# Attention and a cosine feed-forward layer on one core: the short matmuls of a tile in two runs instead of four, and the last rows stored in two halves

## The chip, the cores and the metric

The kernel runs on one core of one Trainium2 chip. Its engines work side by side, each through its own list of instructions in order: TensorE (PE, matmuls, with weight loads as PEld), VectorE (DVE), ScalarE (ACT), GpSimd (POOL) and SyncE (SP, which issues the DMAs here). They wait for each other by semaphores. The metric is device time in microseconds (us): the median of several executions.

## The reference

Chunked attention over 8 batches, 8 heads, 576 positions in chunks of 64, head size 64, and then a feed-forward layer on the result (4608 tokens of 512, inner size 2048), all in float32:

```python
scores = scale * np.matmul(q_c, k_c.transpose(0, 1, 2, 4, 3))   # chunks of 64 x 64
scores = scores - np.max(scores, axis=-1, keepdims=True)
attn = np.exp(scores)
attn = attn / (np.sum(attn, axis=-1, keepdims=True) + 1e-09)
out = np.matmul(attn, v_c)
...
x = np.ascontiguousarray(attn_out.transpose(0, 2, 1, 3)).reshape(B * S, H * D)
...
h = x @ w_in
g = h * np.cos(h)
return (g @ w_out).astype(np.float32)
```

## The kernel before

The 4608 tokens are cut into nine tiles of 512. For each tile, the feed-forward layer goes through sixteen steps, one for each block `fc` of 128 inner columns. To keep float32 precision, every large operand is split into a high and a low part, and three products are added up. A step has these parts:

- `hidden(t, fc)` on TensorE: twelve matmuls of 128 x 512 into a PSUM bank named `h`. The pool `ps_h` has two such banks, used in turn.
- `activated`: six operations, alternately on ScalarE (lines 497, 499, 501) and VectorE (498, 500, 502). They read the bank `h`, form g = h cos h and split it into `g_hi` and `g_lo`. The multiplication in line 500 is the last reader of the bank.
- `project(s)` on TensorE: twelve matmuls that multiply `g` by `w_out` into four banks `acc`, one for each 128 rows (`sub`). It runs LAG = 3 steps behind `hidden`. After the sixteenth step of a tile `finish` copies the four banks out, alternately on ScalarE and VectorE, and stores them.

While a tile goes through its sixteen steps, the attention of the tile after it is worked out in between (`attend`). The eight heads form four pairs `hp` = 0 to 3, and two pairs form a group `g`. The scores of a group are 32 matmuls of 64 x 64, the weighted sums of a group are 32 more. The trace shows two records for each of these short matmuls. They write the two banks `a0` and `a1` (pool `ps_a`); the other six of the eight PSUM banks are `acc` and `h`. The stations of a tile's attention are:

- steps 0 and 1: scores of group 0, then of group 1 (`scores`). The matmuls stand between `hidden` and `project` of the step. VectorE then takes the largest of each row (line 363) and subtracts it (line 367), which empties the banks.
- step 2: exponentials on ScalarE (line 376). Steps 3 to 6: sums and quotients on VectorE.
- steps 4 to 7 and 9 to 12: the weights of each pair are transposed into tiles `pts` by eight VectorE instructions (`turned`, line 422).
- steps 8 and 13: weighted sums of group 0, then of group 1 (`weighted`). ScalarE (line 460) and VectorE (line 463) split the result into the parts `x` that `hidden` reads for the next tile.

The loads for the tile after are issued by SP in program order: values of pairs 2 and 3 at step 9, queries, keys and the other values from step 13 (`prefetch`).

The order of the work comes from two places. The first two and a half tiles (the list `work`, STAGE = 32 steps) are ordered by a planner with estimated durations. From then on a plain loop at the end of the kernel calls the functions; each engine gets its instructions in the order of the calls. Three queues of small pieces hold back work of VectorE and ScalarE: `activate` takes pieces of `soon` and `full` between its own operations, and empties `full`, `soon` and `late`, in that order, at its end. The loop covers the attention of the fourth to ninth tile.

Of the kernel before, what the change touches and what calls it, by code (L numbers as in the profile page):

```python
# [11 lines left out]
F32 = mybir.dt.float32  # L12
# [9 lines left out]
P = 128  # L22
TOK = 512
CH = 64
BL = 32
LAG = 3
# [3 lines left out]
SHIFT = 28  # L30

GROUP = 8

EARLY = 2

# [123 lines left out]
def attention_then_cos_ffn(ctx: ExitStack, tc, qT, kT, v, w_in, w_out, out, wide):  # L159
# [5 lines left out]
    NT, HP = qT.shape[0], qT.shape[1]  # L165
    NFC, NCC = w_in.shape[1], w_in.shape[2]
    DM = out.shape[1]
    NCH = TOK // CH
    NSUB = TOK // P
# [22 lines left out]
    def matmul(*args, **kw):  # L192
        kept(nc.tensor.matmul(*args, **kw))  # L193
# [101 lines left out]

    def load_v(t, hp):

        if t or hp < 2:
            vt = att.tile([P, TOK], F32, name="vt")
        else:  # L300
            if hp == 2:
                values["roomy"] = x_room(1, F32)
            vt = values["roomy"][:, hp - 2]
        load(vt, v[t, hp])
        values[t, hp] = vt

    def bank(kind, i):
        if kind == "a":
            b = ps_a.tile([P, 512], F32, name=f"a{i % 2}")
        else:  # L310
            b = ps_o.tile([P, 512], F32, name=f"acc{i}")
        return b

    def weights_of(t, g):
        if ("e", t, g) not in probs:
            probs["e", t, g] = att.tile([P, 2, NCH, CH], F32, name=f"e{g}", bufs=1)
        return probs["e", t, g]
# [23 lines left out]
    def scores(t, g, banks):  # L341

        for j in range(2):
            qt, kt = queries.pop((t, 2 * g + j))
            for c in range(NCH):
                pr, par = divmod(c, 2)
                cs, ps = slice(c * CH, (c + 1) * CH), slice(par * CH, (par + 1) * CH)
                o = (j * NPR + pr) * CH  # L350
                for h in range(2):
                    hs = slice(h * CH, (h + 1) * CH)
                    matmul(
                        banks[h][ps, o : o + CH], qt[hs, cs], kt[hs, cs], start=True, stop=True
                    )
        e = weights_of(t, g).rearrange("p a (r h) k -> p a r h k", h=2)
        found = []
        for h in range(2):
            sv = banks[h].rearrange("p (a r k) -> p a r k", a=2, k=CH)
            m = att.tile([P, 2, NPR], F32, name="m", bufs=4)  # L360

            def largest(m=m, sv=sv):
                kept(nc.vector.tensor_reduce(out=m, in_=sv, op=ALU.max, axis=AX.X))

            def below(m=m, sv=sv, h=h):
                mb = m.unsqueeze(3).broadcast_to([P, 2, NPR, CH])
                kept(nc.vector.tensor_tensor(e[:, :, :, h], sv, mb, op=ALU.subtract))  # L367

            found.extend((largest, below))
        return found  # L370
# [41 lines left out]

    def turned(t, hp):

        pts = att.tile([P, TOK], F32, name="pts")
        probs[t, hp] = pts
        src = weights_of(t, hp // 2)[:, hp % 2].rearrange("p c (x k) -> p c x k", k=BL)
        dst = pts.rearrange("p (c x q) -> p c x q", x=CH // BL, q=BL)

        def piece(par, qb, kb):  # L420
            i, o = (par * CH + x * BL for x in (qb, kb))
            kept(nc.vector.transpose(out=dst[o : o + BL, :, qb], in_=src[i : i + BL, :, kb]))  # L422

        nb = CH // BL
        return [
            lambda x=(par, qb, kb): piece(*x)
            for par in range(2) for qb in range(nb) for kb in range(nb)
        ]

    def weighted(t, hps, banks):  # L430


        g, first = divmod(hps[0], 2)
        n = len(hps)
        for j, hp in enumerate(hps):
            pts = probs.pop((t, hp))
            vt = values.pop((t, hp))
            for pr in range(NPR):
                for par in range(2):
                    ks = slice(par * CH, (par + 1) * CH)  # L440
                    o = (j * NPR + pr) * CH
                    for h in range(2):
                        hs = slice(h * CH, (h + 1) * CH)
                        fs = slice((2 * pr + h) * CH, (2 * pr + h + 1) * CH)
                        matmul(
                            banks[par][hs, o : o + CH], vt[ks, fs], pts[ks, fs],
                            start=True, stop=True,
                        )
        if (t, g) not in x_parts:
            x_parts[t, g] = tuple(x_room(t, F32R) for _ in range(2))  # L450
        splits = []
        for par in range(2):
            xq = banks[par][:, : n * TOK // 2].rearrange("p (a r q) -> p a r q", a=n, q=CH)
            hi, lo = (
                x[:, first : first + n].rearrange("p a (r c q) -> p a r c q", c=2, q=CH)[:, :, :, par]
                for x in x_parts[t, g]
            )

            def high(xq=xq, hi=hi):
                kept(nc.scalar.copy(out=hi, in_=xq))  # L460

            def rest(xq=xq, hi=hi, lo=lo):
                kept(nc.vector.tensor_tensor(lo, xq, hi.bitcast(F32), op=ALU.subtract))  # L463

            splits.extend((high, rest))
        return splits
# [52 lines left out]
    def project(s):  # L519
        t, fc = order[s]  # L520
        first = s == 0 or order[s - 1][0] != t
        last = s == len(order) - 1 or order[s + 1][0] != t
        g_hi, g_lo = g_parts.pop((t, fc))
        w_hi, w_lo = w_parts["out", fc]
        sums_out = []
        for sub in range(NSUB):
            if first:
                acc[sub] = bank("acc", sub)
            o = acc[sub]
            ss = slice(sub * P, (sub + 1) * P)  # L530
            matmul(o, g_hi[:, ss], w_hi, start=first, stop=False)
            matmul(o, g_hi[:, ss], w_lo, start=False, stop=False)
            matmul(o, g_lo[:, ss], w_hi, start=False, stop=last)
            if last:
                sums_out.append(lambda sub=sub, o=o: finish(t, sub, o, fc == NFC - 1))
        return sums_out

    def out_room(sub):

        return (wts if sub % 2 else dec).tile([P, DM], F32, name=f"half{sub // 2}" if sub % 2 else "w")  # L540

    def finish(t, sub, o, whole):
        r0 = t * TOK + sub * P
        to = out[r0 : r0 + P, :]
        if not whole:

            os, to = att.tile([P, DM], F32, name="vt" if sub % 2 else "pts"), partial[sub]
        elif t == 0:
            os = acc["partial", sub]
        elif t < NT - 1:  # L550
            os = out_room(sub)
        else:
            if sub % 2 == 0:
                acc["last"] = x_room(t + 1, F32)
            os = acc["last"][:, sub % 2]
        if whole and t == 0:
            kept(nc.vector.tensor_tensor(os, os, o, op=ALU.add))
        elif sub % 2 == 0:
            kept(nc.scalar.copy(out=os, in_=o))
        else:  # L560
            kept(nc.vector.tensor_copy(os, o))
        nc.sync.dma_start(out=to, in_=os)
# [9 lines left out]

    def attend(t, step):

        for g in range(2):
            if step == g:
                soon.extend(scores(t, g, (bank("a", 0), bank("a", 1))))
            if step == 8 + 5 * g:
                late.extend(weighted(t, (2 * g, 2 * g + 1), (bank("a", 0), bank("a", 1))))
        if step == 9:  # L580
            for hp in range(2, HP):
                load_v(t, hp)
        if step == 3:
            soon.extend(lambda hp=hp: total(t, hp) for hp in range(HP))
            soon.append(lambda: inverse(t))

        for hp in {4: (0, 1), 5: (2,), 6: (3,)}.get(step, ()):
            soon.append(lambda hp=hp: quotient(t, hp))
        if 4 <= step < 8 or 9 <= step < 13:
            hp, odd = divmod(step - 4 - (step > 8), 2)  # L590
            if not odd:
                pieces["turn"] = turned(t, hp)
            soon.extend(pieces["turn"][4 * odd : 4 * odd + 4])

    def prefetch(t):
        for hp in range(HP):
# [253 lines left out]
        work[i][2]()  # L850


    for s in range(STAGE, len(order) + LAG):
        if s < len(order):
            t, fc = order[s]
            h = hidden(t, fc)
            if t + 1 < NT:
                attend(t + 1, fc)
            if fc == NFC - 3 and t + 2 < NT:
                prefetch(t + 2)  # L860
        full.extend(project(s - LAG))
        if s < len(order):
            activate(t, fc, h)
            if t + 1 < NT and fc == 2:
                exponentials(t + 1)
        take(full, len(full))
# [54 lines left out]
```

## Time and profile before

| | us |
|---|---|
| median of 3 executions | 859.04 (858.68 to 859.16) |
| the profiled execution | 858.76 |
| its span, first to last instruction | 857.0 |
| TensorE busy | 841.9 |
| VectorE busy | 553.4 |
| ScalarE busy | 390.4 |

The span is what the profiler sees of one execution; the remaining 1.76 us of that execution lie around it. Line numbers in the profile are those of the kernel before; every matmul has the line of a small helper, L193, so matmuls are told apart by the tiles that they write: `h`, `acc` and `a`. In a row of the timeline the first number is the start, the second the length of the group, and `x12` the number of instructions. Matmuls overlap: the length of a group holds the whole last matmul, so the distance of two starts says what a group costs.

### The profile page before, as it was taken

The page shows a single profiled execution, that of the slowest core. Times are in us where ns is not written, and L with a number is a line of the kernel's source. Part 1 is how long each engine was busy: PE and PEld are TensorE (multiplying, and loading weights), DVE is VectorE, ACT ScalarE, POOL GpSimd, SP SyncE. Part 2 cuts the span into 40 slices and gives each one's busy share as a digit, 9 for nine tenths or more (in the row PEclk, how much of TensorE's full clock was granted, in tenths as well). Part 3 has the DMA queues.
Part 4 walks back from the last instruction along what each step waited for, and adds up shares of the span by engine and source line. Part 5 has one row for each costly group of instructions (what it writes and reads, how often), then busy time and mean ns, then how long its engine had stood idle before and what let it go on. Part 6 is the DMA issues. An engine that isn't in the chain of part 4 may idle for free.

```text
span 857.0 us, 14052 instructions
## 1 busy us (share of the span) xinstructions
PE 841.9 (98%) x5792; PEld 692.2 (81%) x5792; DVE 553.4 (65%) x942; ACT 390.4 (46%) x636; POOL 6.8 (1%) x12
## 2 busy tenths in 40 slices
PE   5999999999999999999999999999999999999998
PEld 4778888888888888888888888888888888888886
DVE  6979888744776468655776567645865676634332
ACT  5999963433533343333533353335333353333332
POOL 1010000000000000000000000000000000000000
PEclk9999999999999999999999999999999999999999
DMA  9990200420112010300130011201030010001001
GB/s 337 413 413 18 75 1 1 148 99 1 50 31 92 26 50 1 124 25 2 49 124 25 2 50 49 76 26 50 1 123 25 2 49 25 1 1 49 1 1 49
DMA packets 26559, 57.52 MB, mean 67 GB/s; under 512 B 2944, under 2 KB 2944, under 8 KB 26496
## 3 DMA queue, kind: packets, MB, share of 16 engines
q1 hardware_dynamic: 26496, 56.63, 18.3%
q8 instruction: 45, 0.74, 0.4%
q14 instruction: 18, 0.15, 0.1%
HBM read 46.14 MB, written 10.49 MB: 66 GB/s over the span
## 4 chain that ended last, share of the span: by engine, by line
PE 91%; ACT 4%; DMA 2%; DVE 1%; issue 0%; SPq 0%; ACTq 0%
PE acc L193 45%; PE h L193 43%; PE a L193 4%; DMA qt<-in_qT_dram 2%; ACT half L262 1%; DMA w_in<-in_w_in_dram 1%; ACT w L260 1%; ACT g L499 0%; ACT w_out L270 0%; ACT w_in L270 0%; ACT L376 0%; ACT g_hi L501 0%; SPq L190 0%; DVE g L498 0%; ACT e L376 0%
## 5 line engine op out<-in xcount | busy, mean ns | idle before, releaser
L193 PE MATMUL h<-x,w_in 128*128 128x512 f32 x1728 | 416.0, 390 | 0.4 <-DVE g L500 0.4
L193 PEld LDWEIGHTS h<-x,w_in 128*128 128x128 f32 x1728 | 323.8, 188 | 68.5 <-DVE g L500 1.4
L193 PE MATMUL acc<-w_out,g_hi 128*128 128x512 f32 x1152 | 358.3, 392 | 0.0
L193 PEld LDWEIGHTS acc<-w_out,g_hi 128*128 128x128 f32 x1152 | 214.0, 188 | 45.3
L193 PE MATMUL acc<-w_out,g_lo 128*128 128x512 f32 x576 | 224.4, 390 | 0.0
L498 DVE SCALAR_TENSOR_TENSOR g<-g,h 128x512 f32<-128x512 int32 x144 | 98.6, 685 | 141.3 <-ACT g L497 140.5
L497 ACT ACTIVATE g<-h 128x512 int32<-128x512 f32 x144 | 86.0, 597 | 194.6 <-PE h L193 194.2
L502 DVE TENSOR_TENSOR g_lo<-g,g_hi 128x512 fp32r<-128x512 f32 x144 | 99.5, 691 | 78.3 <-ACT g_hi L501 75.1
L501 ACT CAST g_hi<-g 128x512 fp32r<-128x512 f32 x144 | 89.4, 621 | 128.0 <-DVE g L500 80.6
L499 ACT ACTIVATE g<-g 128x512 f32<-128x512 f32 x144 | 91.0, 632 | 120.2 <-DVE g L498 120.1
L500 DVE TENSOR_TENSOR g<-h,g 128x512 f32<-128x512 f32 x144 | 99.5, 691 | 54.1 <-ACT g L499 50.9
L193 PEld LDWEIGHTS acc<-w_out,g_lo 128*128 128x128 f32 x576 | 108.1, 188 | 22.7
L422 DVE STREAM_TRANSPOSE pts<-e 32x256 f32<-32x256 f32 x224 | 97.3, 435 | 3.7
L386 DVE TENSOR_REDUCE z<-e 128x8 f32<-128x512 f32 x36 | 23.8, 679 | 3.8 <-ACT e L376 3.8
L193 PEld LDWEIGHTS a<-kt,qt 64*64 64x64 f32 x1024 | 18.3, 135 | 6.4 <-issue 5.7
L376 ACT ACTIVATE e<-e 128x1024 f32<-128x1024 f32 (+1 forms) x22 | 19.1, 899 | 9.2 <-DVE e L337 9.1
L255 DVE SCALAR_TENSOR_TENSOR w<-w,half 128x512 uint32<-128x512 uint32 x32 | 21.7, 686 | 2.3 <-ACT half L262 1.2
L463 DVE TENSOR_TENSOR x<-a,x 128x512 fp32r<-128x512 f32 (+1 forms) x36 | 22.1, 654 | 0.6 <-ACT x L460 0.5
L193 PEld LDWEIGHTS a<-pts,vt 64*64 64x64 f32 x1056 | 17.0, 134 | 5.6 <-issue 4.9
L193 PE MATMUL a<-kt,qt 64*64 64x64 f32 x1024 | 20.6, 221 | 0.6 <-DVE x L463 0.6
L396 DVE TENSOR_TENSOR e<-e,z 128x512 f32<-128x512 f32 x30 | 20.3, 683 | 0.0
L367 DVE TENSOR_TENSOR e<-a,m 128x512 f32<-128x512 f32 x28 | 19.1, 686 | 0.5
(50 smaller groups left out, 246.6 us busy)
## 6 DMA issues: line engine op xcount, KB each, us to landing
qt<-in_qT_dram SPq DMA_DIRECT2D x36, 256.0 KB, 5.2
kt<-in_kT_dram SPq DMA_DIRECT2D x36, 256.0 KB, 5.3
vt<-in_v_dram SPq DMA_DIRECT2D x34, 256.0 KB, 3.5
w_in<-in_w_in_dram SPq DMA_DIRECT2D x16, 512.0 KB, 9.6
w_out<-in_w_out_dram SPq DMA_DIRECT2D x16, 512.0 KB, 9.9
out_dram<-w SPq DMA_DIRECT2D x16, 256.0 KB, 2.1
out_dram<-half SPq DMA_DIRECT2D x16, 256.0 KB, 2.1
out_dram<-x SPq DMA_DIRECT2D x4, 256.0 KB, 2.0
```

Source lines behind the costliest of these rows:

```text
L193: kept(nc.tensor.matmul(*args, **kw))
L255: kept(nc.vector.scalar_tensor_tensor(bits, bits, 3, low, op0=ALU.logical_shift_left, op1=ALU.bitwise_or))
L386: kept(nc.vector.tensor_reduce(out=sums_of(t)[:, hp], in_=weights_of(t, hp // 2)[:, hp % 2], op=ALU.add, axis=AX.X))
L396: kept(eng.tensor_tensor(e, e, zb, op=ALU.mult))
L422: kept(nc.vector.transpose(out=dst[o : o + BL, :, qb], in_=src[i : i + BL, :, kb]))
L463: kept(nc.vector.tensor_tensor(lo, xq, hi.bitcast(F32), op=ALU.subtract))
L497: lambda: kept(nc.scalar.activation(n, h, AF.Identity, bias=0.25, scale=0.5 / math.pi)),
L498: lambda: kept(nc.vector.scalar_tensor_tensor(g, n, -2.0 * math.pi, h, op0=turns, op1=over)),
L499: lambda: kept(nc.scalar.activation(g, g, AF.Sin, bias=0.5 * math.pi)),
L500: lambda: kept(nc.vector.tensor_tensor(g, h, g, op=ALU.mult)),
L501: lambda: kept(nc.scalar.copy(out=g_hi, in_=g)),
L502: lambda: kept(nc.vector.tensor_tensor(g_lo, g, g_hi.bitcast(F32), op=ALU.subtract)),
```

## The change

In the loop, `attend` no longer issues matmuls. A new function `burst` does it twice a tile: the scores of all four pairs in step 0 (SCORES), and the weighted sums of all four pairs in step 12 (WEIGHTED). Group 0 writes one bank `h` and `a0`, group 1 the other bank `h` and `a1`. The pieces that empty the banks go to `late`, those of the two `h` banks ahead of the others.

```diff
+SCORES = 0
+WEIGHTED = 12
...
     def attend(t, step):
-        for g in range(2):
-            if step == g:
-                soon.extend(scores(t, g, (bank("a", 0), bank("a", 1))))
-            if step == 8 + 5 * g:
-                late.extend(weighted(t, (2 * g, 2 * g + 1), (bank("a", 0), bank("a", 1))))
...
-        if 4 <= step < 8 or 9 <= step < 13:
-            hp, odd = divmod(step - 4 - (step > 8), 2)
+        if 4 <= step < 12:
+            hp, odd = divmod(step - 4, 2)
...
+    def burst(t, step):
+        banks = [(ps_h.tile([P, 512], F32, name="h"), bank("a", g)) for g in range(2)]
+        if step == SCORES:
+            first, second = (scores(t, g, banks[g]) for g in range(2))
+        else:
+            first, second = (weighted(t, (2 * g, 2 * g + 1), banks[g]) for g in range(2))
+        late.extend(first[:2] + second[:2] + first[2:] + second[2:])
```

In the loop, `project` of the step comes ahead of the run, and the next `project` is drawn forward to stand behind it, so that in the step after it there is none:

```diff
+    through = STAGE - 1 - LAG
     for s in range(STAGE, len(order) + LAG):
...
-            if fc == NFC - 3 and t + 2 < NT:
+            if fc == WEIGHTED + 1 and t + 2 < NT:
                 prefetch(t + 2)
-        full.extend(project(s - LAG))
+        if s - LAG > through:
+            through += 1
+            full.extend(project(through))
+        if s < len(order) and t + 1 < NT and fc in (SCORES, WEIGHTED):
+            burst(t + 1, fc)
+            through += 1
+            full.extend(project(through))
```

All four pairs' weights and values now wait for one run, so they need more room. For pairs 2 and 3 of these tiles, the values go into rooms of the queries (`qt`, four of them, free after the scores), and the transposed weights into the tile that held the weights of group 0:

```diff
     def load_v(t, hp):
-        if t or hp < 2:
+        if t > 2 and hp >= 2:
+            vt = att.tile([P, TOK], F32, name="qt", bufs=HP)
+        elif t or hp < 2:
...
     def turned(t, hp):
-        pts = att.tile([P, TOK], F32, name="pts")
+        if t > 2 and hp >= 2:
+            pts = weights_of(t, 0)[:, hp % 2].rearrange("p c k -> p (c k)")
+        else:
+            pts = att.tile([P, TOK], F32, name="pts")
```

Last, in the very last `project` the fourth bank (`sub` 3) is filled in two halves of 256 columns, each with its three matmuls, its copy and its store; the first half is copied by VectorE, the second by ScalarE:

```diff
+            n = DM // 2 if s == len(order) - 1 and sub == NSUB - 1 else DM
+            for a in range(0, DM, n):
+                cs = slice(a, a + n)
+                matmul(o[:, cs], g_hi[:, ss], w_hi[:, cs], start=first, stop=False)
+                matmul(o[:, cs], g_hi[:, ss], w_lo[:, cs], start=False, stop=False)
+                matmul(o[:, cs], g_lo[:, ss], w_hi[:, cs], start=False, stop=last and a + n == DM)
+                if last:
+                    sums_out.append(lambda sub=sub, o=o, cs=cs: finish(t, sub, o, fc == NFC - 1, cs))
...
-        elif sub % 2 == 0:
+        elif sub % 2 == 0 or cs.start:
             kept(nc.scalar.copy(out=os, in_=o))
```

How the instructions move is seen in their order on each engine. The first place is on TensorE, the scores of one tile. `kt` and `qt` are keys and queries, `a_4601` and `a_4602` the two banks `a` in step 0, `a_4676` and `a_4677` the same banks in step 1; in brackets is what a row waits for. Before, the run of group 0 stands between `h` and `acc` of step 0, that of group 1 between `h` and `acc` of step 1:

```order
L193 MATMUL h<-x_4473,w_in_335 128x512
L193 MATMUL a_4601<-kt,qt 64x64 [waits DMAHW1_49,DMAHW0_49,PE_49]
L193 MATMUL a_4602<-kt,qt 64x64 [waits PE_49]
...
L193 MATMUL acc_4004<-w_out_1410,g_hi 128x512 x2
...
L193 MATMUL h<-x_4473,w_in_427 128x512
L193 MATMUL a_4676<-kt,qt 64x64 [waits DMAHW4_49,DMAHW5_49,DVE_49,PE_49]
L193 MATMUL a_4677<-kt,qt 64x64 [waits DVE_49,PE_49]
...
L193 MATMUL acc_4004<-w_out_1448,g_hi 128x512 [waits Activation_49]
```

Now, behind `acc` of an older step, group 0 writes one bank `h` and `a_3815`, and right behind it group 1 the other bank `h` and `a_3817`. Then come the next `acc` and two `h` in a row:

```order
L196 MATMUL h<-kt,qt 64x64 [waits DMAHW1_49,DMAHW0_49,DVE_49]
L196 MATMUL a_3815<-kt,qt 64x64
...
L196 MATMUL h<-kt,qt 64x64 [waits DMAHW5_49,DMAHW4_49,DVE_49]
L196 MATMUL a_3817<-kt,qt 64x64 [waits PE_49]
...
L196 MATMUL acc_3207<-w_out_1448,g_hi 128x512 [waits Activation_49]
...
L196 MATMUL h<-x_3614,w_in_427 128x512 [waits DVE_49,PE_49]
...
L196 MATMUL h<-x_3614,w_in_491 128x512 [waits DVE_49,PE_49]
```

The two runs have become one, and the DVE wait in its middle is for the multiplication that last reads this step's `h`.

The second place is on VectorE, the steps 0 and 1 of the same kind of tile. Before, the four largest (`m<-a`) and differences (`e<-a,m`) of a step stand among its own three operations:

```order
L498 SCALAR_TENSOR_TENSOR g<-g,h 128x512 [waits Activation_49]
L363 TENSOR_REDUCE m<-a_4601 128x8 [waits PE_49]
L500 TENSOR_TENSOR g<-h,g 128x512 [waits Activation_49]
L367 TENSOR_TENSOR e_4635<-a_4601,m 128x8x64 [waits DVE_49]
L502 TENSOR_TENSOR g_lo<-g,g_hi 128x512 [waits PE_49,Activation_49]
L363 TENSOR_REDUCE m<-a_4602 128x8
L367 TENSOR_TENSOR e_4635<-a_4602,m 128x8x64 [waits DVE_49]
```

Now all eight stand behind the three operations of step 0, the `h` banks first:

```order
L509 TENSOR_TENSOR g<-h,g 128x512 [waits Activation_49]
L511 TENSOR_TENSOR g_lo<-g,g_hi 128x512 [waits PE_49,Activation_49]
L368 TENSOR_REDUCE m<-h 128x8 [waits PE_49]
L372 TENSOR_TENSOR e_4643<-h,m 128x8x64 [waits DVE_49]
L368 TENSOR_REDUCE m<-h 128x8 [waits PE_49]
L372 TENSOR_TENSOR e_4678<-h,m 128x8x64 [waits DVE_49]
L368 TENSOR_REDUCE m<-a_4608 128x8
L372 TENSOR_TENSOR e_4643<-a_4608,m 128x8x64 [waits DVE_49]
L368 TENSOR_REDUCE m<-a_4610 128x8 [waits PE_49]
L372 TENSOR_TENSOR e_4678<-a_4610,m 128x8x64 [waits DVE_49]
L507 SCALAR_TENSOR_TENSOR g<-g,h 128x512 [waits Activation_49]
```

Step 1 (the last row) comes behind them and has none of its own.

The third place is the end of the program on ScalarE. Before, its last rows are the copies of the banks `sub` 0 and 2, each waiting for TensorE:

```order
L497 ACTIVATE g<-h 128x512 [waits PE_49,Activation_49]
L499 ACTIVATE g<-g 128x512 [waits DVE_49]
L501 CAST g_hi<-g 128x512 [waits DVE_49,PE_49]
L559 COPY x_7549<-acc_7080 128x512 [waits PE_49]
L559 COPY x_7554<-acc_7088 128x512 [waits PE_49]
```

Now the second half of `sub` 3 (`acc_7080` here) comes behind them:

```order
L508 ACTIVATE g<-g 128x512 [waits DVE_49]
L510 CAST g_hi<-g 128x512 [waits DVE_49,PE_49]
L573 COPY x_7540<-acc_7068 128x512 [waits PE_49]
L573 COPY x_7545<-acc_7076 128x512 [waits PE_49]
L573 COPY x_7545<-acc_7080 128x256 [waits DVE_49]
```

It waits for VectorE, whose last copy is the first half of the same bank.

More of the change, by code (lines that the diff above doesn't have):

```diff
@@ L530, in project @@
             ss = slice(sub * P, (sub + 1) * P)
[L531 to L535, printed above, removed]
+            n = DM // 2 if s == len(order) - 1 and sub == NSUB - 1 else DM
[6 more added lines that the diff above has]
+                    sums_out.append(lambda sub=sub, o=o, cs=cs: finish(t, sub, o, fc == NFC - 1, cs))
         return sums_out
@@ L540, in out_room, with finish @@
         return (wts if sub % 2 else dec).tile([P, DM], F32, name=f"half{sub // 2}" if sub % 2 else "w")
-    def finish(t, sub, o, whole):
+    def finish(t, sub, o, whole, cs):
         r0 = t * TOK + sub * P
-        to = out[r0 : r0 + P, :]
+        to = out[r0 : r0 + P, cs]
         if not whole:
@@ L554, in finish @@
                 acc["last"] = x_room(t + 1, F32)
-            os = acc["last"][:, sub % 2]
+            os = acc["last"][:, sub % 2, cs]
+        o = o[:, cs]
         if whole and t == 0:
             kept(nc.vector.tensor_tensor(os, os, o, op=ALU.add))
-        elif sub % 2 == 0:
+        elif sub % 2 == 0 or cs.start:
             kept(nc.scalar.copy(out=os, in_=o))
```

## The prediction, made before the change was run

> **What bounds the kernel now.** I read the page first (busy time, then the chain that ended last), then busy time by stretches, then TensorE's timeline around the short matmuls.
>
> ```profile
> PE 841.9 (98%) x5792; PEld 692.2 (81%) x5792; DVE 553.4 (65%) x942; ACT 390.4 (46%) x636; POOL 6.8 (1%) x12
> PE 91%; ACT 4%; DMA 2%; DVE 1%; issue 0%; SPq 0%; ACTq 0%
> ```
>
> TensorE is busy 98% of the span and makes up 91% of the chain. A busy PE need not be a useful one, so the next view cuts the loop into whole tiles.
>
> ```profile
> core 0: us, PE busy (x) PEld busy (x) DVE busy (x) ACT busy (x) POOL busy (x), PEclk, DMA share, GB/s
> 299.04:391.37 92.33, 92.33 (x642) 75.89 (x640) 60.49 (x104) 36.91 (x58) 0.00 (x0) 1.00 0.14 47
> 391.37:483.69 92.32, 92.32 (x642) 75.89 (x640) 60.49 (x104) 36.90 (x58) 0.00 (x0) 1.00 0.14 46
> ```
>
> One tile takes 92.32 us; the granted clock is 1.00. VectorE has 60.5 of these, ScalarE 36.9: both have room. What the 92.32 us consist of stands in TensorE's timeline (start, length, engine, operation; x12 are twelve matmuls).
>
> ```profile
> 337.11 2.88 PE L193 MATMUL h<-x,w_in 128*128 128x512 f32 x12
> ...
> 342.55 2.88 PE L193 MATMUL h<-x,w_in 128*128 128x512 f32 x12
> 345.36 1.18 PE L193 MATMUL a<-pts,vt 64*64 64x64 f32 x64
> 346.47 0.73 PE L193 MATMUL acc<-w_out,g_hi 128*128 128x512 f32 x2
> ...
> 349.33 2.88 PE L193 MATMUL h<-x,w_in 128*128 128x512 f32 x12
> ...
> 388.73 2.88 PE L193 MATMUL h<-x,w_in 128*128 128x512 f32 x12
> 391.54 1.16 PE L193 MATMUL a<-kt,qt 64*64 64x64 f32 x64
> 392.63 0.73 PE L193 MATMUL acc<-w_out,g_hi 128*128 128x512 f32 x2
> ...
> 395.49 2.88 PE L193 MATMUL h<-x,w_in 128*128 128x512 f32 x12
> ```
>
> A step without short matmuls lasts 342.55 - 337.11 = 5.44 us: 2.72 for `h` and 2.72 for `acc`. A step with a run of them lasts 349.33 - 342.55 = 6.78 (weighted sums) or 395.49 - 388.73 = 6.76 (scores). So one run costs 1.34 or 1.32, say 1.33. Sixteen steps and four runs: 16 x 5.44 + 4 x 1.33 = 92.36, the 92.32 of the stretch. **Inside a tile TensorE waits for nothing that could be removed; only what a run costs can be saved.** (A run is 32 matmuls; the trace has two records for each, hence x64.)
>
> **The term that pays: the fixed part of a run.** Two looks at the same run, ending at 345.60 and at 346.30, count the records begun by then:
>
> ```profile
> 345.36 0.45 PE L193 MATMUL a<-pts,vt 64*64 64x64 f32 x15
> 345.36 1.15 PE L193 MATMUL a<-pts,vt 64*64 64x64 f32 x62
> ```
>
> From 345.60 to 346.30 there began 62 - 15 = 47 records, one each 14.9 ns. From the whole run, (1.18 - 0.22) / 63 = 15.2 ns (0.22 is the last record's own length). Then 64 records are 0.95 to 0.97 us, and of 1.33 us 0.36 to 0.38 belong to entering and leaving the run. It can be seen: the last `h` matmul has its turn until 342.55 + 2.72 = 345.27, the run begins at 345.36 (0.09 late); its last record begins about 346.32, the first `acc` matmul at 346.47 (0.14 later than the next record would); and the twelve `acc` matmuls take 349.33 - 346.47 = 2.86 instead of 2.72 (0.14). Sum 0.37.
>
> The change makes of 24 runs of 64 records 12 runs of 128: same number of records, 12 entries and exits fewer. 12 x 0.37 = **4.4 us** gained. Bounds: if the change of banks in the middle of a long run costs what the entry does (0.09), 0.28 x 12 = 3.4 us remain; if the records come at 14.5 ns, 0.40 x 12 = 4.8 us are gained.
>
> **What is moved, and what covers it.** Call T the end of `h` of the step with the run (391.45 in the rows above). Now `acc` of an older step comes first, then the run, so the run starts at T + 2.72 + 0.09 and its second half at about T + 3.78. The first half writes the bank that the step before left, the second half the bank of this step's `h`, which must have been read. The last reader is the multiplication on VectorE:
>
> ```profile
> 391.70 0.60 ACT L497 ACTIVATE g<-h 128x512 int32<-128x512 f32 x1 [2.02 <-PE h L193]
> 392.33 0.69 DVE L498 SCALAR_TENSOR_TENSOR g<-g,h 128x512 f32<-128x512 int32 x1 [1.92 <-ACT g L497]
> 393.06 0.63 ACT L499 ACTIVATE g<-g 128x512 f32<-128x512 f32 x1 [0.76 <-DVE g L498]
> 393.72 0.69 DVE L500 TENSOR_TENSOR g<-h,g 128x512 f32<-128x512 f32 x1
> 839.62 2.88 PE L193 MATMUL h<-x,w_in 128*128 128x512 f32 x12
> 846.06 0.69 DVE L502 TENSOR_TENSOR g_lo<-g,g_hi 128x512 fp32r<-128x512 f32 x1 [0.74 <-ACT g_hi L501]
> L363 DVE TENSOR_REDUCE m<-a x28: 681/684/686, 110.4 to 680.5; 128x8 f32<-128x512 f32 x28
> L367 DVE TENSOR_TENSOR e<-a,m x28: 679/682/694, 112.2 to 681.2; 128x512 f32<-128x512 f32 x28
> ```
>
> The multiplication ends at 394.41 = T + 2.96: 0.8 us before it is needed. **Cost 0, cover 0.8.** The same holds for step 12.
>
> Then the four banks must be emptied. VectorE's remainder of the step ends at T + 4.41 (846.75, in a step without other work whose `h` ended at 839.62 + 2.72 = 842.34); the largest and the difference of the first bank take 0.68 + 0.68: bank free at T + 5.8, the second at T + 7.2. The `h` that write them begin at T + 2.72 + 2.28 + 2.72 = T + 7.7 and T + 10.4. Cost 0, cover 1.9 and 3.2. After the weighted sums ScalarE and VectorE share it (0.58 and 0.68 each), which ends sooner.
>
> The older `acc` that follows the run is missing one step later, so two `h` stand next to each other and ScalarE, whose chain of a step takes 3.7 us (to 846.03, where L502 begins), comes 1.0 us late to the second (step 2), and with it the exponentials and step 3. In the trace step 3's bank is free at 415.60 and the `h` that writes it starts 2.97 later:
>
> ```profile
> 414.91 0.69 DVE L500 TENSOR_TENSOR g<-h,g 128x512 f32<-128x512 f32 x1 [0.66 <-ACT g L499]
> ...
> 418.57 2.88 PE L193 MATMUL h<-x,w_in 128*128 128x512 f32 x12
> ```
>
> 2.0 of it are left. Cost 0. The transposes of a tile now stand in steps 4 to 11 without the gap at 8; per step VectorE has 3 x 0.69 + 4 x 0.44 = 3.8 of 5.44 us.
>
> Loads: values 2 and 3 lie in `qt` rooms, so the last two query loads of the next tile wait in SP's queue for the weighted run, with the loads behind them. One issue is 0.43, a landing 5.2:
>
> ```profile
> 439.33 0.43 SPq L190 DMA_DIRECT2D qt<-in_qT_dram  x1
> qt<-in_qT_dram SPq DMA_DIRECT2D x36, 256.0 KB, 5.2
> ```
>
> Six issues and a landing are some 8 us; from the weighted run to the next scores there are eight pieces of 2.72, 21.8 us. Cost 0, cover 13.
>
> **The end.** The last 128 rows go out in two halves of 256 columns.
>
> ```profile
> 853.42 0.69 DVE L561 COPY x<-acc 128x512 f32<-128x512 f32 x1 [0.67 <-PE acc L193]
> 852.00 2.48 SPq L562 DMA_DIRECT2D out_dram<-x  x4
> out_dram<-x SPq DMA_DIRECT2D x4, 256.0 KB, 2.0
> L460 ACT CAST x<-a x36: 367/583/606, 17.7 to 748.1; 128x512 fp32r<-128x512 f32 x32, 128x256 fp32r<-128x256 f32 x4
> L463 DVE TENSOR_TENSOR x<-a,x x36: 415/682/692, 18.3 to 749.0; 128x512 fp32r<-128x512 f32 x32, 128x256 fp32r<-128x256 f32 x4
> L193 PEld LDWEIGHTS acc<-w_out,g_hi 128*128 128x128 f32 x1152 | 214.0, 188 | 45.3
> 50.92 1.03 PE L405 MATMUL a<-ident,e 128*128 128x128 f32 x8
> ```
>
> Before: one copy of 0.69, the store's issue, 2.0 us. After, the order shows VectorE's half waiting for TensorE's last matmul and ScalarE's half waiting for VectorE's: they share a bank and do not overlap. The 256-column forms took 0.415 and 0.367; with a hand-over of 0.04 (393.02 to 393.06 above) that is 0.82 against 0.69, **0.13 us lost**. The last store is half as large; its landing lies between 1.0 and 2.0, and I take 2.0, the only row there is. Six matmuls of 256 columns take the time of three of 512 if the weight loads keep up: between no loss and 6 x 0.188 - 0.68 = 0.45; I take none, since the transposes pass one such load each (1.03 - 0.27) / 7 = 0.11 us. Bounds of the end: -0.85 to +0.60.
>
> **Sum.** -4.4 + 0.13 = -4.27 us. The profiled execution took 858.76 us (span 857.0 and 1.76 around it), so 854.5; the runs' median, 859.04, lies 0.28 above it, so **854.8**.
>
> **Rivals.** (A) *A long run slows down past the 64th record.* No row shows more than 64 short records on end. If TensorE is fed from a store filled during the long matmuls, the second half comes at the rate of supply. Against it: 15 records in the first 0.24 us and 47 in the next 0.70 show no slowing inside 64. For a price, the slowest row of short matmuls:
>
> ```profile
> 21.01 2.08 PE L193 MATMUL a<-kt,qt 64*64 64x64 f32 x64 [0.57 <-DVE x L463]
> q8 instruction: 45, 0.74, 0.4%
> ```
>
> It is (2.08 - 0.22) / 63 = 30 ns a record, 15 more: 12 x 64 x 0.015 = 11.6 us, so 859.04 - 4.27 + 11.6 = 866.4. This decides from 4.27 / 768 = 5.6 ns more per record, 20.6 ns. [...]
> [...] The measurement decides, and the sum stands.
>
> (B) *The wait for `h` takes the place.* If ScalarE comes to step 0 or 12 later than in the rows above, the second half waits for the multiplication. The cover is 0.8; 1.0 late costs 0.2 in each of 12 runs, 2.4 us, so 857.2; beyond 1.2 late the gain is gone. Against it: ScalarE idled 2.02 us before that step's first instruction, and nothing is put ahead of it.
>
> (C) *There is nothing fixed to save*: what I read as entry and exit comes back at the change of banks in mid-run, where a run has waits as well. Then only the end is left, 859.2. Against it: the 0.28 us at the exit stand where matmuls of another shape follow, which the middle of a run lacks.
>
> **Chances.** Forecast 0.73 (853.4 to 856.2 by the bounds: 859.04 - 4.8 - 0.85, 859.04 - 3.4 + 0.6); B 0.09 (856.2 to 857.8, a little of it beyond); C 0.09; A 0.09. The range reaches over the forecast and B, 853.2 to 857.8. A measurement of this kernel can tell some 0.2% from no change, 1.7 us: faster means below 857.3, which takes in the forecast and most of B, 0.80; same is C and the rest of B, 0.11; slower is A, 0.09.
>
> **What would show it.** In the profile after: twelve runs x128 in the loop, 2.1 to 2.2 us wide (127 x 15 ns + 0.22), tiles of 92.32 - 0.74 = 91.6 us; no waits of TensorE's loads for DVE L509 in mid-run; the two `h` after the scores next to each other without a gap; a last copy that ends 0.13 us later after the last matmul. A run wider than 2.6 us speaks for A, a gap at its 64th record for B, tiles of 92.3 for C. The prediction would be wrong if the exit's cost grew with the length of the run, which no row here can show.

## The result, and the profile after the change

| | before | after |
|---|---|---|
| median of 4 executions | 858.86 us (858.17 to 859.16) | 854.12 us (853.43 to 854.40) |
| span of the profiled execution | 857.0 | 852.3 |
| its mean granted clock | 0.999 | 0.998 |

The ratio of the times is 0.9945, with a 95% interval of 0.9928 to 0.9962: the kernel became faster by 4.7 us, where 4.27 were forecast. Two executions far off the rest, one of 937.39 us at a granted clock of 0.85 and one of 2181.83 us of the kernel before, are left out of all medians here.

The page of the kernel after, its busy times and the shares of the chain that ended last:

```profile
span 852.3 us, 14049 instructions
PE 839.6 (99%) x5795; PEld 694.5 (81%) x5795; DVE 554.1 (65%) x942; ACT 389.3 (46%) x637; POOL 6.8 (1%) x12
PE 93%; ACT 4%; DVE 1%; DMA 1%; issue 0%; POOL 0%; SPq 0%; ACTq 0%; POOLq 0%
```

TensorE is still the bound, now with 93% of the chain, with three matmuls more than before (the three that are cut in two at the end). So the gain isn't work left out; the same matmuls take less time. Two tiles of the loop show where (busy times in each stretch, the granted clock behind them):

```profile
core 0: us, PE busy (x) PEld busy (x) DVE busy (x) ACT busy (x) POOL busy (x), PEclk, DMA share, GB/s
279.22:370.76 91.54, 91.54 (x641) 75.83 (x641) 60.66 (x105) 36.70 (x58) 0.00 (x0) 1.00 0.13 47
370.76:462.31 91.55, 91.55 (x642) 75.83 (x641) 60.70 (x105) 36.70 (x58) 0.00 (x0) 1.00 0.14 47
```

A tile takes 91.55 us instead of 92.32, at the same clock: 0.77 less. Six tiles of the loop have the change, and 6 x 0.77 = 4.62 of the 4.7 by which the span became shorter. Two runs fewer in a tile, so one entry and exit was worth 0.385 us.

TensorE's timeline around a merged run of weighted sums (start, length, engine, line, operation; x2 are two records in a row):

```profile
363.14 2.88 PE L196 MATMUL h<-x,w_in 128*128 128x512 f32 x12
365.86 0.61 PE L196 MATMUL acc<-w_out,g_hi 128*128 128x512 f32 x2
...
368.67 0.27 PE L196 MATMUL h<-pts,vt 64*64 64x64 f32 x2
368.68 0.27 PE L196 MATMUL a<-pts,vt 64*64 64x64 f32 x2
368.77 0.23 PE L196 MATMUL h<-pts,vt 64*64 64x64 f32 x2
...
368.83 0.23 PE L196 MATMUL h<-pts,vt 64*64 64x64 f32 x2
...
369.61 0.23 PE L196 MATMUL a<-pts,vt 64*64 64x64 f32 x2
369.65 0.23 PE L196 MATMUL h<-e,qt 64*64 64x64 f32 x2
...
370.52 0.23 PE L196 MATMUL h<-e,qt 64*64 64x64 f32 x2
370.54 0.23 PE L196 MATMUL a<-e,qt 64*64 64x64 f32 x2
370.69 0.73 PE L196 MATMUL acc<-w_out,g_hi 128*128 128x512 f32 x2
...
373.55 0.62 PE L196 MATMUL h<-x,w_in 128*128 128x512 f32 x2
```

`acc` now comes first; its last matmul has its turn until 365.86 + 2.72 = 368.58, and the run begins at 368.67. Its second half (from `e,qt`, whose tiles hold the weights and values of pairs 2 and 3) begins at 369.65, 0.04 after the row before it, as elsewhere in the run: no gap in mid-run, and no slowing. The first 64 records take 369.65 - 368.67 = 0.98 us; from 369.65 to 370.52 there begin 60 more, one each 14.5 ns. The whole run is 370.54 + 0.23 - 368.67 = 2.10 us wide. Then `acc` begins at 370.69, and these twelve matmuls take 373.55 - 370.69 = 2.86 us.

### The profile page after: what moved, and what is told of

Read it like the earlier page. It is cut to its first block, busy times and chain, and to the rows that moved or that the text cites. A ratio compares the mean times of both kernels' runs of the same rounds, so it can differ in the third digit from the quotient of the medians.

```text
span 852.3 us, 14049 instructions
## 1 busy us (share of the span) xinstructions
PE 839.6 (99%) x5795; PEld 694.5 (81%) x5795; DVE 554.1 (65%) x942; ACT 389.3 (46%) x637; POOL 6.8 (1%) x12
## 4 chain that ended last, share of the span: by engine, by line
PE 93%; ACT 4%; DVE 1%; DMA 1%; issue 0%; POOL 0%; SPq 0%; ACTq 0%; POOLq 0%
PE h L196 47%; PE acc L196 45%; PE a L196 2%; ACT half L265 1%; DMA kt<-in_kT_dram 1%; ACT w L263 0%; ACT x L469 0%; ACT w_out L273 0%; ACT L381 0%; ACT g_hi L510 0%; ACT g L508 0%; ACT e L381 0%; DVE x L472 0%; ACT w_in L273 0%; POOL e L401 0%
## 5 line engine op out<-in xcount | busy, mean ns | idle before, releaser
L431 DVE STREAM_TRANSPOSE pts<-e 32x256 f32<-32x256 f32 x128 | 55.5, 435 | 2.0
L431 DVE STREAM_TRANSPOSE e<-e 32x256 f32<-32x256 f32 x96 | 41.8, 435 | 1.8
L472 DVE TENSOR_TENSOR x<-a,x 128x512 fp32r<-128x512 f32 (+1 forms) x24 | 14.4, 639 | 0.6 <-ACT x L469 0.5
L196 PEld LDWEIGHTS h<-kt,qt 64*64 64x64 f32 x384 | 11.7, 135 | 2.1 <-issue 2.1
```

## The experiments

All start from the changed kernel. The first three kernels here ran several times, beside the kernel before with a median of 858.93 us. The last six ran once each; beside them the kernel before took 858.56 (with the first four of the six) and 859.44 (with the last two), so their times are sure to about 1 us.

**The theory:** the whole gain is the fixed cost of entering and leaving a run of short matmuls, and it is to be had only because `acc` stands ahead of the run (so that the second half finds its bank read) and behind it (so that the banks are emptied in time). **The rivals:** it comes from something else in the change (other banks, the other order on VectorE and ScalarE, two `h` side by side), or from the end of the program.

### The changed kernel again

No edit; it is the measure for the other runs.

> The changed kernel once more, as the measure for the runs beside it on the same chip. Both theories: 4 to 5 us under the kernel before; tiles of 91.55 us and a span of 852 to 853 us in the profile.

Measured: 853.95 us, ratio 0.9946 (0.9926 to 0.9966), span 852.1. The result repeats.

### The runs apart again, all else kept

The second `acc` is moved between the two halves of the run. Banks, tiles, transposes, loads and the end stay as the change has them, but there are 24 runs of 64 records again.

```diff
-    def burst(t, step):
+    def burst(t, step, between):
...
+        for g in range(2):
...
+            if g == 0:
+                between()
...
-            burst(t + 1, fc)
             through += 1
-            full.extend(project(through))
+            burst(t + 1, fc, lambda: full.extend(project(through)))
```

> The changed kernel with one thing undone: the second acc of the step, which stood behind the run, now stands between the two groups, so that there are two runs of 64 records again, in the same step, with the same banks, the same order of evacuation and the same rooms. Theory (a run has a fixed part of 0.37 us, for entering and leaving it): 12 entries and exits more, 12 x 0.37 = 4.4 us more than the changed kernel, tiles of 92.3 us, so about 858.5. Rival (the gain comes from the banks, from the order of the pieces or from the two h in a row): within 1 us of the changed kernel, tiles of 91.55 to 91.7 us. Both expect no new wait: the second group's banks are free 2 us before the h that write them.

Measured: 859.09 us, 1.0005 (0.9995 to 1.0014) of the kernel before, span 857.1. Two places in the chain, both the two `h` behind the weighted sums, are one tile apart:

```profile
282.50 5.69 PE h L196 x24
...
374.89 5.69 PE h L196 x24
```

A tile takes 374.89 - 282.50 = 92.39 us instead of 91.55. The gain is gone, and all of it: 857.1 - 852.1 = 5.0 us by the spans for 12 entries and exits, 0.42 each (0.43 by the medians). No new wait shows in its place: among the eleven longest of the list of waits (9.5 us or more in total each) none is TensorE's, and in TensorE's timeline both runs of the weighted sums begin 0.09 us late, at 369.69 (369.37 + 0.23 = 369.60 is the end of the turn of the `acc` ahead) and at 373.73 (373.41 + 0.23 = 373.64), with no wait beside them. That the tile is 0.07 longer than the 92.32 of the kernel before stays unexplained. The rival that saw the gain in banks or order falls, since this kernel has both; so does the forecast's rival C, that a run has nothing fixed to save.

### The last rows whole

```diff
-            n = DM // 2 if s == len(order) - 1 and sub == NSUB - 1 else DM
+            n = DM
```

> The changed kernel with the last 128 rows in one piece, as before the change. Theory (the end is neither a gain nor a loss that counts: a copy that ends 0.14 us later against a last store that is half as large): within 0.3 us of the changed kernel; in the trace the last copy ends 0.72 us after the last matmul, not 0.86, and the span goes on for 2.9 us after it, not 2.7. Rival (the halves brought a part of the 4.7 us, since the last store is half as large): 1 us or more above the changed kernel.

Measured: 853.73 us, ratio 0.9940 (0.9926 to 0.9955), span 852.1, like that of the changed kernel beside it. The two halves at the end bring nothing that can be measured, and cost nothing. The end of the changed kernel's timeline shows why:

```profile
848.45 0.28 PE L196 MATMUL acc<-w_out,g_lo 128*128 128x256 f32 x1
848.76 0.42 DVE L575 COPY x<-acc 128x256 f32<-128x256 f32 x1 [0.70 <-PE acc L196]
849.22 0.37 ACT L573 COPY x<-acc 128x256 f32<-128x256 f32 x1 [0.58 <-DVE x L575]
```

In the kernel with whole rows it is one copy:

```profile
848.15 0.39 PE L196 MATMUL acc<-w_out,g_lo 128*128 128x512 f32 x1
848.58 0.69 DVE L575 COPY x<-acc 128x512 f32<-128x512 f32 x1 [0.67 <-PE acc L196]
```

With halves the last copy ends 849.59 - 848.73 = 0.86 us after the last matmul, with whole rows 849.27 - 848.54 = 0.73. But from the copy to the end of the span it is 852.3 - 849.59 = 2.71 with halves and 852.1 - 849.27 = 2.83 with whole rows: the smaller store gives back what the second copy costs.

### The run ahead of both acc

```diff
+        run = s < len(order) and t + 1 < NT and fc in (SCORES, WEIGHTED)
+        if run:
+            burst(t + 1, fc)
         if s - LAG > through:
...
-        if s < len(order) and t + 1 < NT and fc in (SCORES, WEIGHTED):
-            burst(t + 1, fc)
+        if run:
```

> The changed kernel with the run ahead of both acc of its step (h, run, acc, acc instead of h, acc, run, acc). Theory (the second half of a run waits for the multiplication that last reads this step's h, done 2.97 us after the end of h, and the older acc hides that wait): the second half would be due 0.09 + 0.97 = 1.06 us after h, so it waits 1.9 to 2.0 us in each of 12 runs: 23 us more than the changed kernel, about 877, and the trace shows waits of TensorE for DVE L511 or its neighbour in mid-run. Rival (the place of the run does not matter, the older acc is there only for the order of g): within 1 us of the changed kernel.

Measured: 887.21 us, span 885.4. In the list of waits (total us, times, the longest) stands what the older `acc` had hidden:

```profile
PE h L196 <- DVE g L509: 21.4, 13, 1.8
```

Twelve of the thirteen are in the runs. The run's second group cannot begin until the multiplication in line 509 has read this step's `h`:

```profile
665.39 0.22 PE L196 MATMUL a<-pts,vt 64*64 64x64 f32 x2
667.37 0.27 PE L196 MATMUL h<-e,qt 64*64 64x64 f32 x2 [1.76 <-DVE g L509]
```

The list counts from the end of the row ahead; from start to start it is 667.37 - 665.39 = 1.98. The waits are as expected, but the time is 33.1 us longer than the changed kernel's by the spans, not 23. The chain shows the rest; two places of the same kind, both the two `acc` behind a run:

```profile
572.79 5.66 PE acc L196 x24
...
669.11 6.63 PE acc L196 x24
```

From one run of weighted sums to the next it is 95.73 us (from 282.51 to 378.24 in the chain) where nothing more happens: 4.18 over the changed kernel's 91.55, so 2.09 a run and 25.1 in twelve. At five of the twelve runs the two `acc` behind take 6.43 to 6.63 instead of 5.66, and they begin 0.6 later (474.55 - 378.24 = 96.31 in the chain, against 95.73). About 1.5 us each, 7.7 in all: 25.1 + 7.7 = 32.8 of the 33.1. There the granted clock had fallen: the three stretches of some 96 us that hold these five places have 0.98, 0.97 and 0.96, those with the other seven 1.00. At one of the five it was 0.50 for 2 us (the number behind the busy times; the stretch lies over the end of the run whose second half starts at 667.37, and over the `acc` behind it):

```profile
668.00:670.00 2.00, 2.00 (x45) 1.75 (x39) 0.00 (x0) 0.00 (x0) 0.00 (x0) 0.50 0.23 72
```

### No acc drawn forward behind the run

```diff
             burst(t + 1, fc)
-            through += 1
-            full.extend(project(through))
```

> The changed kernel without the second acc drawn forward: the next h follows the run at once, and acc comes in its usual turn. Theory (the first bank is free 5.7 to 5.8 us after the end of h, and that next h would be due 5.1 us after it): a wait of 0.6 to 0.8 us behind each of the six score runs, 0.2 to 0.5 behind the six runs of weighted sums, 5 to 8 us more than the changed kernel, about 860. Rival (the evacuation is fast enough anyway): within 1 us of the changed kernel.

Measured: 863.18 us, span 861.4, 9.1 longer than the changed kernel's. The next `h` now follows the run at once and finds its bank unread. In the list of waits:

```profile
PE h L196 <- DVE e L372: 5.8, 6, 1.0
PE h L196 <- DVE x L472: 2.8, 6, 0.5
```

After the scores (L372 empties the bank) that is 1.0 us a run, after the weighted sums (L472) 0.5; the sum, 8.6, is nearly all of the 9.1. The expectation was 5 to 8, somewhat too little.

### Short runs added: the fixed part by itself

In steps 5 to 10 of six tiles, 36 places in all, a short run is added between `h` and `acc`, into a bank `a` that nobody reads: work that the reference doesn't have. The first kind is of the form of the real ones, two float32 matmuls of 64 x 64, which are four records in the trace.

```diff
+    def extra():
+        b = bank("a", 0)
+        for j in range(2):
+            hs = slice(j * CH, (j + 1) * CH)
+            matmul(b[hs, :CH], ident[:CH, hs], ident[:CH, :CH], start=True, stop=True)
...
+            if t + 1 < NT and 5 <= fc < 11:
+                extra()
```

> The changed kernel with 36 very short runs added: in the steps 5 to 10 of six tiles, between h and acc, two float32 matmuls of 64 x 64 (four records) whose result nothing reads. Theory (the fixed part belongs to entering and leaving the 64 x 64 form, whatever the length): 36 x (0.37 + 4 x 0.015) = 15.5 us more than the changed kernel, about 869.6. Rival (the cost of a run grows with its records alone): 36 x 4 x 0.0207 = 3.0 us more, about 857.

Measured: 871.93 us, span 870.2: 17.8 more than the 854.12 of the changed kernel, for 36 places, 0.49 each. Less four records at 0.015 that leaves 0.43 us of fixed cost, though hardly any work is done. Timeline of such a step, TensorE and its weight loads:

```profile
340.17 2.88 PE L196 MATMUL h<-x,w_in 128*128 128x512 f32 x12
342.98 0.33 PE L196 MATMUL a<-ident 64*64 64x64 f32 x4
343.24 0.73 PE L196 MATMUL acc<-w_out,g_hi 128*128 128x512 f32 x2
...
346.09 1.29 PE L196 MATMUL h<-x,w_in 128*128 128x512 f32 x5
...
342.98 0.20 PEld L196 LDWEIGHTS a<-ident 64*64 64x64 f32 x4 [0.35 <-issue]
343.24 0.30 PEld L196 LDWEIGHTS acc<-w_out,g_hi 128*128 128x128 f32 x2
```

The run begins 342.98 - (340.17 + 2.72) = 0.09 late, `acc` 0.26 after it, and the twelve `acc` matmuls take 346.09 - 343.24 = 2.85. The weight loads begin together with their matmuls, on the way in and on the way out: none was fetched ahead.

The second kind has the same number of records, but all 128 weights across and 64 columns; so the form of the weights is that of the neighbours and only the length is short.

```diff
+            cs = slice(j * CH, (j + 1) * CH)
+            matmul(b[:, cs], ident, ident[:, cs], start=True, stop=True)
```

> The same 36 places, but the two float32 matmuls use the whole array (128 x 128 weights, 64 columns), so that only the type changes against their neighbours, not the 64 x 64 form. Theory (the gaps at entry and exit belong to the 64 x 64 form): no gap of 0.09 ahead and none of 0.14 behind, only the records themselves at some 0.11 us each and perhaps the slower following group: 36 x 0.45 to 0.55 = 16 to 20 us more, with the records next to their neighbours. Rival (the gaps belong to float32 beside the rounded type of the long matmuls): the same gaps as with 64 x 64, and 36 x (0.45 + 0.23) = 24 us or more.

Measured: 871.74 us, span 870.0: 17.6 for 36, again 0.49 each, but made up in another way.

```profile
339.61 2.89 PE L196 MATMUL h<-x,w_in 128*128 128x512 f32 x12
342.33 0.56 PE L196 MATMUL a<-ident 128*128 128x64 f32 x4
342.70 0.70 PE L196 MATMUL acc<-w_out,g_hi 128*128 128x512 f32 x2
...
342.10 0.65 PEld L196 LDWEIGHTS a<-ident 128*128 128x128 f32 x4
342.67 0.30 PEld L196 LDWEIGHTS acc<-w_out,g_hi 128*128 128x128 f32 x2
```

The run begins at 339.61 + 2.72 = 342.33, to the hundredth: no gap. Its load begins 0.23 ahead. Four records of this form take 342.70 - 342.33 = 0.37, and that is where most of the time goes; their loads take 0.65, of which 0.23 lie ahead, so the records can hardly come faster. Yet the `acc` behind is slow here too: in the step before, from 336.76 to 339.61, 2.85.

That left the question what makes the following group slow. These runs had float32 operands, their neighbours a rounded type, so the next kernel took the rounded operands of the neighbours, four matmuls of 128 x 128 weights and 64 columns:

```diff
+            matmul(b[:, cs], w_parts["in", fc][0][:, :P], x_parts[t, 0][0][:, 0, cs], start=True, stop=True)
```

> The same 36 places with four short matmuls of the whole array (128 x 128 weights, 64 columns) in the rounded type of their neighbours: neither the type nor the form changes, and there are four records as in the other two. Theory (in a tile of the kernel the acc group behind a run takes 0.13 us longer because float32 records stand ahead of it, and the gaps at entry and exit belong to the 64 x 64 form): no gaps, the next group 2.72 us, so only the records, each bounded by its weight load, 36 x 4 x 0.09 to 0.19 = 13 to 27 us more. Rival (the slower group follows from any run of short matmuls, since weight loads are then no longer ahead of the matmuls): the group behind takes 2.82 us or more here too.

Measured: 871.10 us, span 869.3: 17.0 more for 36, 0.47 each.

```profile
342.43 0.53 PE L196 MATMUL a<-x,w_in 128*128 128x64 f32 x4
342.79 0.71 PE L196 MATMUL acc<-w_out,g_hi 128*128 128x512 f32 x2
...
345.62 1.75 PE L196 MATMUL h<-x,w_in 128*128 128x512 f32 x7
```

The group behind takes 345.62 - 342.79 = 2.83. The theory that the change of type makes it slow would have had 2.72 and falls: **here a run of short matmuls makes the next group some 0.11 to 0.14 us slower, in both forms and both types.** By what means the runs don't show. The traces say where: nearly all of it lies at the head of the group, whose third matmul begins 0.54 to 0.57 after the first in the four kernels with short runs, and 0.45 in an undisturbed group (366.31 - 365.86 in the changed kernel). There the group's first weight load begins with its matmul or 0.03 ahead (342.67 against 342.70 above), where in an undisturbed group it begins 0.23 ahead (343.87 against 344.10 in the changed kernel). That the late load is the cause is likely, but no run separates the two.

Last, the fourth corner: the rounded type, but 64 x 64 weights.

```diff
+            matmul(b[:CH, cs], w_parts["in", fc][0][:CH, hs], x_parts[t, 0][0][:CH, 0, cs], start=True, stop=True)
```

> The same 36 places with four short matmuls of 64 x 64 in the rounded type: the form changes, the type does not. Theory (entry and exit belong to the form): a gap of about 0.09 ahead and 0.14 behind, as with float32 in the 64 x 64 form, in each of the 36 places, so 36 x 0.23 = 8 us and the records themselves. Rival (the gaps need the change of type as well): no gaps, the records alone.

Measured: 874.75 us, span 872.7: 20.6 more for 36, 0.57 each.

```profile
340.49 2.88 PE L196 MATMUL h<-x,w_in 128*128 128x512 f32 x12
343.30 0.42 PE L196 MATMUL a<-x,w_in 64*64 64x64 f32 x4
343.65 0.73 PE L196 MATMUL acc<-w_out,g_hi 128*128 128x512 f32 x2
...
343.30 0.30 PEld L196 LDWEIGHTS a<-x,w_in 64*64 64x64 f32 x4 [0.35 <-issue]
```

The gap at the entry is back (343.30 against 340.49 + 2.72 = 343.21), and so is the load that begins no earlier than its matmul. At the exit the last record, 0.22 long, begins at 343.30 + 0.42 - 0.22 = 343.50, and `acc` 0.15 later; with float32 it was 0.15 as well (342.98 + 0.33 - 0.22 = 343.09, then 343.24). In the two kernels with 128 x 128 weights `acc` follows at the records' own pace (0.37 and 0.36 us after the start of the four records). So of the four kinds the two of 64 x 64 have the gaps and the two of 128 x 128 haven't: they belong to the change of form, not to the type. They are 0.09 us on the way in and 0.15 on the way out; what TensorE does in them no run here shows.

## Why the prediction was right, step by step

**The bound** was read rightly: TensorE waits for nothing inside a tile, so only what a run costs could be saved, and that is where the time came from (4.62 of 4.7 in the tiles).

**The fixed part of a run** was the right mechanism and a little small in size. Forecast was 0.37, at most 0.40; the tiles gave 0.385, the kernel with the runs apart 0.42, the short runs 0.43. What it left out can be seen at the head of a run: its second `h` row begins at 368.77, 0.10 after the first, the third 0.06 later, as all others do. Together: entry 0.09, this 0.04, exit 0.11 (370.69 less 370.52 + 0.06, where the next row would begin), the slower group behind 0.14 (2.86 less 2.72); 0.38. The prediction named three of these four parts, and the short runs show that entry and exit belong to the 64 x 64 form and the slower group to the short runs of either form. That the exit grows with the run's length, by which the forecast would have been wrong, did not come: 0.11 after 128 records (0.125 if it is read as the prediction read it, from the start of the last record), where 0.14 had been read after 64.

**The second half needs the multiplication; cover 0.8.** The step with the scores has its `h` from 387.15 to 387.15 + 2.72 = 389.87, which is T here; the other rows are VectorE's:

```profile
387.15 2.88 PE L196 MATMUL h<-x,w_in 128*128 128x512 f32 x12
...
392.15 0.69 DVE L509 TENSOR_TENSOR g<-h,g 128x512 f32<-128x512 f32 x1 [0.70 <-ACT g L508]
...
394.91 0.69 DVE L372 TENSOR_TENSOR e<-h,m 128x512 f32<-128x512 f32 x1
...
396.23 0.69 DVE L372 TENSOR_TENSOR e<-h,m 128x512 f32<-128x512 f32 x1
```

The multiplication ends at 392.84 = T + 2.97, where 2.96 was forecast. Rival B (a wait in mid-run) needed it 0.8 later and didn't come. The kernel with the run ahead of both `acc` is B made real: 2.09 us a run, five times what the merging saves.

**The banks are emptied in time.** The first bank is free at 395.60 = T + 5.7, the second at 396.92 = T + 7.05 (forecast 5.8 and 7.2). TensorE's timeline has the two `h` that write them back to back:

```profile
397.56 5.60 PE L196 MATMUL h<-x,w_in 128*128 128x512 f32 x24
403.00 0.62 PE L196 MATMUL acc<-w_out,g_hi 128*128 128x512 f32 x2
```

They begin at 397.56 = T + 7.7 and 2.72 later, with 2.0 and 3.4 us to spare (forecast 1.9 and 3.2), and 403.00 - 397.56 = 5.44 for 24 matmuls leaves no room for a gap. This cover is bought by the `acc` drawn forward: without it the wait is 1.0 and 0.5 us.

**Two `h` side by side, ScalarE late.** Forecast was that of 2.97 us of slack 2.0 are left for the bank of step 3. Its last reader now is a row of VectorE's timeline, and the `h` that writes it again one of TensorE's:

```profile
413.60 0.69 DVE L509 TENSOR_TENSOR g<-h,g 128x512 f32<-128x512 f32 x1 [0.66 <-ACT g L508]
...
416.60 2.88 PE L196 MATMUL h<-x,w_in 128*128 128x512 f32 x12
```

416.60 - 414.29 = 2.3 us are left. Cost 0, as said. For the loads, too, no wait shows: the two tiles above are alike to 0.01 us.

**The end** was the one step with the wrong result. "0.13 us lost" holds for the copies (0.86 against 0.73 after the last matmul), but the landing of the last store had been taken at 2.0, the only row there was, and the smaller store comes in 0.12 sooner. Nothing is lost or gained; the sum was 0.13 too low for it, inside its bounds.

**Rival A**, that a long run slows down past the 64th record, falls: 14.5 ns a record in the second half against 0.98 us / 64 = 15.3 in the first.

The forecast of 854.8 was 0.7 above the 854.12 measured. Some 0.2 of it are the fixed part (12 x 0.015), 0.13 the end, 0.18 that the kernel before now has a median of 858.86 instead of 859.04; the rest is within what such medians vary.

## What to carry to other kernels

Where TensorE is the bound, count how often it goes into a run of small matmuls and out again: here each time cost about 0.4 us, as much as 26 of the matmul records, so fewer and longer runs pay even though no work is saved. Such a merging needs more banks at once, and was worth having here only with a group of other matmuls ahead of the run, which gives the banks time to be read, and one behind it, which gives them time to be emptied; without the one this kernel lost 33 us, without the other 9, for a gain of 4.7. Weighted sums and the next tile's scores in one run might save one more entry a tile; that was not tried.

## What was not expected of the hardware

When the run stood ahead of both `acc`, TensorE waited some 1.8 us (21.4 in all) at twelve runs, each time between short matmuls of 64 x 64. In the one execution that was timed, about 1.5 us more was lost at each of five of these runs, in stretches with a granted clock of 0.96 to 0.98 (0.50 for 2 us at one of them); the stretches with the other seven have 1.00, like the tiles of the changed kernel, which has no such wait. Whether the wait brings the clock down, and why at five and not at seven, this run doesn't show. So here a wait of 1.8 us of TensorE went with a loss of up to 1.8 + 1.5 = 3.3, and a forecast that counts only the wait, as the expectation of that run did, was too low.

The second was the slower group behind any short run: twelve matmuls of 128 x 512 that take 2.83 to 2.86 us instead of 2.72, even where the short matmuls are of their own form and type.
